# Two layers of sliding attention and an MLP mixer: the first group's w3 product in fp16, block 0's x centred by VectorE, and a new order

## The chip, the cores and the metric

The kernel runs on one core of one Trainium2 chip. The metric is device time in microseconds (us) of that core for one launch. Lower is better.

## The reference

x has 2048 rows (tokens) of 512 columns in fp32. Two different layers, A and B, are applied in turn, twice, with the same weights both times:

```python
x = A_x
x = x + A(LN(x), wqkv, wo)
x = x + B(LN(x), w1, w2, w3, w4)
x = x + A(LN(x), wqkv, wo)
x = x + B(LN(x), w1, w2, w3, w4)

def A(x, wqkv, wo):            # 32 heads of 16 columns
    q, k, v = split(x @ wqkv)  # 512 x 1536
    # row s attends to rows s, s-2, ..., s-14 (8 keys, those below 0 masked)
    return softmax(q . k[s - 2w] / 4) . v[s - 2w] @ wo

def B(x, w1, w2, w3, w4):      # called with LN(x), and normalises again
    h  = gelu(LN(x) @ w1)      # 512 x 512
    hs = shift(h) @ w2         # quarters of the columns shifted by +1, -1, +2, -2 rows
    x1 = x + hs
    return x1 + gelu(LN(x1) @ w3) @ w4   # 512 x 1792, 1792 x 512
```

LN subtracts the row's mean and divides by the root of its variance plus 1e-5; it has no gain or bias. All inputs and the output are fp32.

## The kernel before

**Tiles and stages.** The 2048 rows are four blocks of 512, and a block is four tiles of 128 rows. With two layers there are eight passes over a block, numbered n = 0 to 7 (0 to 3 are the blocks of the first layer). One pass goes through five stages, each a function of that name: `p1` (LN, transpose of x, the q, k, v products with wqkv), `p2` (attention, on VectorE with some help from GpSimd; `p2_unit` takes one or two of the four quarters of a block), `p3` (product with wo, residual, LN, product with w1, gelu, the row shift), `p4` (product with w2, residual, LN, transpose) and `p5` (w3, gelu, w4, residual). Because of the row shift a pass can finish only part of its rows: `p5` of n = 0 has three tiles, its last has five, the others four. `p5` walks over 14 chunks of 128 of the 1792 columns of w3; the result of a chunk's first (up) product goes through gelu and into the second (down) product, which adds up in PSUM (`acc`).

**Precision.** Nearly all products are three fp16 products in place of one fp32 product. Each operand is cut into a high half (its fp16 rounding) and a low half (the fp16 rounding of the remainder), and `HLS` lists the three pairs high-high, high-low and low-high:

```python
HLS = ((0, 0), (0, 1), (1, 0))
```

Weights are scaled per row by a power of two before the cut, with a factor found from their sum of squares (`small_weight` for wqkv, wo, w1, w2; `big_pair` for w3 and w4). The halves of w3 and w4 are kept in DRAM (`w34_d`) and each `p5` loads them chunk by chunk. Two places use plain fp32 matmuls: the qkv product of block 0 (`p1_quarters`, which takes wqkv quarter by quarter as it arrives), and the whole of `p5` for the first pass (`n < PLAIN`, `PLAIN = 1`, function `plain_chunk`), whose w3 and w4 are read in fp32 from the inputs.

**Normalisation at the start.** `p1_norm` takes mean and variance of an x tile on VectorE (BN_STATS, BN_AGGR). For block 0 GpSimd then does three small operations (`power`: variance plus eps, the power -1/2, minus mean times root) and one pass over the tile, x times root minus mean times root (`normed`). TensorE transposes the tile (`turn_f32`), ScalarE copies it out of PSUM, and the qkv products follow. ScalarE's copy of q out of PSUM multiplies by 1/4.

**Transposes elsewhere.** A tile that needs its fp16 halves transposed goes either through TensorE (`turn_pe`, `turn_f32`) or as a transposing DMA (`turn_dma`: ScalarE writes the fp16 copy, VectorE or GpSimd the remainder, the SP queue issues the transpose). `BY_DMA` says from which n on a stage uses the DMA.

**What sets the order.** The program is first recorded as a list of operations, each with a sort key, an engine (some with a second one) and the buffers it reads and writes. `PLACES` is a table with one integer per operation, which replaces the key; `OTHER` names the operations that run on their second engine. `plan` walks the operations in that order, assigns a slot of a pool to each buffer (`mm` and `acc` four PSUM banks each, `w` eight weight slots, `g` five, `f32` six) and emits the instructions. All instructions are recorded through one helper, `InOrder.issue`, so every row of the profile names its line, L338. Each engine runs its own list strictly in that order, and waits when an input is not there. Nearly all DMAs are issued from the SP queue, whose list is in the table's order too.

**Loads at the start.** The loads that are not needed for block 0's qkv products carry `begun`, a dependence on the copy of block 0's first quarter. `small_weight` loads a 512 x 512 weight with one DMA. `big_pair` converts two chunks of w3 and the same two of w4 together, seven times; one operation, `scales`, waits for all of them and computes the factors `s_w3`, `c_g`, `s_w4` that undo the scaling.

## Time and the profile before

| | us |
|---|---|
| median of 3 runs | 1144.0 (1142.68 to 1894.58) |
| the profiled execution | 1145.03 |
| its span, first to last instruction | 1143.2 |
| TensorE (PE) busy | 1124.1 (98%) |
| VectorE (DVE) busy | 862.6 (75%) |
| ScalarE (ACT) busy | 618.6 (54%) |
| GpSimd (POOL) busy | 417.9 (37%) |
| mean granted TensorE clock | 0.997 |

"Span" is the time between the first and the last instruction of one execution; the profiled execution's own time is 1.8 us longer. PE are the matmuls, PEld the weight loads beside them, SPq the SP queue's DMA issues. A row of the timeline has the start and the duration in us, the engine, the operation, "out<-in" by the program's names, partitions x elements, and in brackets the idle time ahead of it and what ended that. A row of a group has count, busy time in us, mean ns of one, and idle time ahead. A row of the waits has who waits for whom: the total in us, how often, the longest. A row of the busy windows has the stretch, its length, and the busy time of PE, PEld, DVE, ACT and POOL in it with the count of instructions, then the granted clock, the busy share of the DMA engines, and GB/s.

### The profile page before, as it was taken

How to read it: one execution, taken by the hardware profiler on the slowest of the kernel's cores; microseconds unless marked ns; L12 is line 12 of the kernel's file. 1: busy time of each engine (PE TensorE's matmuls, PEld its weight loads, DVE VectorE, ACT ScalarE, POOL GpSimd, SP SyncE). 2: the span in 40 equal slices, each digit the busy share in tenths (PEclk: the TensorE clock that was granted, in tenths of full speed). 3: DMA queues.
4: the chain of work that ended last, by engine and by line, in shares of the span. 5: the costliest groups of instructions: out<-in, count | busy, mean ns of one | idle time of the engine just before them, and what ended most of it. 6: DMA issues, size and time to landing. Idle time of an engine off the chain costs nothing.

```text
span 1143.2 us, 15112 instructions
## 1 busy us (share of the span) xinstructions
PE 1124.1 (98%) x5190; PEld 532.4 (47%) x5190; DVE 862.6 (75%) x919; ACT 618.6 (54%) x1089; POOL 417.9 (37%) x596
## 2 busy tenths in 40 slices
PE   8989999999999999999999999999999999999998
PEld 6544445554444444444444444444444444444554
DVE  4989899997899998988888888378986888323212
ACT  4766785247863565464654565354555554535321
POOL 4342364125652571135534353252324342322000
PEclk9999999999999999999999999999999999999999
DMA  6988989997989669974679756596687865524322
GB/s 175 217 205 215 223 216 259 256 238 182 265 234 222 162 161 211 244 187 121 161 182 230 192 136 166 128 237 177 154 206 166 199 168 158 113 75 112 100 88 79
DMA packets 249165, 206.37 MB, mean 181 GB/s; under 512 B 131032, under 2 KB 192472, under 8 KB 249088
## 3 DMA queue, kind: packets, MB, share of 16 engines
q1 hardware_dynamic: 247472, 203.63, 72.3%
q10 hardware_dynamic: 1616, 1.77, 0.5%
q8 instruction: 41, 0.67, 0.2%
q14 instruction: 36, 0.29, 0.1%
HBM read 132.64 MB, written 37.87 MB: 149 GB/s over the span
## 4 chain that ended last, share of the span: by engine, by line
PE 60%; ACT 2%; DVE 1%; issue 1%; POOL 1%; POOLq 0%; DVEq 0%; ACTq 0%
PE mm L338 42%; PE acc L338 18%; POOL small L338 1%; ACT f L338 1%; DVE L L338 0%; DVE prod L338 0%; ACT junk L338 0%; DVE f L338 0%; ACT L338 0%; ACT g L338 0%; ACT mm L338 0%; POOL f L338 0%; DVE x L338 0%; POOL o L338 0%; DVE h L338 0%
## 5 line engine op out<-in xcount | busy, mean ns | idle before, releaser
L338 PE MATMUL acc<-w,g 128*128 128x512 f16 (+1 forms) x1260 | 307.3, 394 | 0.0
L338 PE MATMUL mm<-nT,w 128*128 128x512 f16 (+1 forms) x1288 | 301.7, 389 | 0.8 <-ACT f L338 0.8
L338 PE MATMUL mm<-wq_hl,xt 128*128 128x512 f16 x1008 | 226.8, 381 | 3.2 <-DMA xt<-f 2.3
L338 ACT ACTIVATE mm<-mm,s_w 128x512 f32<-128x512 f32 (+1 forms) x144 | 89.7, 628 | 195.0 <-PE mm L338 194.7
L338 PEld LDWEIGHTS <-w 128*128 128x128 f16 x1344 | 125.2, 98 | 142.2 <-issue 1.0
L338 PEld LDWEIGHTS <-g 128*128 128x128 f16 x1176 | 114.7, 98 | 137.5
L338 DVE TENSOR_TENSOR prod<-kv,L 128x2048 f32<-128x2048 f32 x64 | 148.7, 2325 | 13.6 <-POOL o L338 12.2
L338 PEld LDWEIGHTS <-xt 128*128 128x128 f16 x1008 | 98.8, 98 | 122.5 <-issue 4.8
L338 DVE TENSOR_REDUCE L<-prod 128x128 f32<-128x2048 f32 x64 | 146.2, 2284 | 1.2
L338 POOL TENSOR_SCALAR small<-small 128x1 f32<-128x1 f32 (+1 forms) x200 | 88.8, 444 | 137.8 <-ACT junk L338 123.8
L338 DVE TENSOR_TENSOR prod<-kv,q 128x2048 f32<-128x2048 f32 x58 | 134.3, 2316 | 3.7 <-DMA q<-q_d 1.9
L338 DVE TENSOR_TENSOR prod<-prod 128x512 f32<-128x512 f32 (+2 forms) x109 | 111.5, 1026 | 2.7
L338 POOL TENSOR_TENSOR g<-f,g 128x512 f16<-128x512 f32 x39 | 54.8, 1409 | 117.8 <-ACT g L338 69.2
L338 DVE SCALAR_TENSOR_TENSOR g<-mm,c_g,g 128x512 f16<-128x512 f32 x56 | 41.5, 745 | 63.7 <-ACT g L338 63.7
L338 PE MATMUL mm<-w_hl,h 128*128 128x512 f16 x384 | 85.7, 379 | 1.1 <-POOL h L338 1.1
L338 PE MATMUL mm<-nT,w_hl 128*128 128x512 f16 x384 | 86.5, 379 | 0.0
L338 POOL TENSOR_TENSOR small<-small,nhalf 128x1 f32<-128x1 f32 (+1 forms) x104 | 72.3, 695 | 8.7
L338 PE MATMUL mm<-wo_hl,oT 128*128 128x512 f16 x336 | 74.3, 379 | 0.0
L338 POOL TENSOR_TENSOR prod<-prod 128x512 f32<-128x512 f32 (+1 forms) x24 | 30.5, 1271 | 105.9 <-DVE prod L338 99.4
L338 ACT ACTIVATE ev<-mm,s_kv 128x512 f32<-128x512 f32 x56 | 38.1, 681 | 54.8 <-PE mm L338 40.0
L338 ACT ACTIVATE g<-mm,c_g 128x512 f16<-128x512 f32 x98 | 66.6, 684 | 1.9
L338 PEld LDWEIGHTS <-oT 128*128 128x128 f16 x426 | 41.5, 98 | 49.0 <-issue 0.6
(188 smaller groups left out, 1217.8 us busy)
## 6 DMA issues: line engine op xcount, KB each, us to landing
w<-w SPq DMA_DIRECT2D x196, 256.0 KB
kv<-kv_d SPq DMA_DIRECT2D x112, 352.0 KB
w<-in_B_w_dram SPq DMA_DIRECT2D x56, 256.0 KB
kv_d<-ev SPq DMA_DIRECT2D x112, 128.0 KB
q_d<-ev SPq DMA_DIRECT2D x28, 256.0 KB
w<-g SPq DMA_DIRECT2D x28, 256.0 KB
q<-q_d SPq DMA_DIRECT2D x28, 256.0 KB
x<-x SPq DMA_DIRECT2D x26, 256.0 KB
```

What stands on the lines that cost most here:

```text
L338: i = f(*a, **k).ins
```

## The change

The numbers of `PLACES` and `OTHER` are all new, and several functions change:

- **The first pass's up product** (`p5`, `n < PLAIN`) takes the halves of w3 from `w34_d`, as the other passes do, and makes 12 fp16 matmuls of 384 columns for a chunk (4 row chunks of w3, three pairs each) where 4 fp32 matmuls stood. Its gelu undoes the scaling with `s_w3`. The down product stays fp32 with w4 from the input (`plain_down`).
- **Block 0's second normalised x** (`p4`, n = 0) is therefore cut into fp16 halves and transposed by DMA (`BY_DMA["p4"]` 1 to 0), not by TensorE in fp32.
- **Block 0's first x** is centred only: x minus mean, by VectorE (or GpSimd, by `OTHER`; one tile of four is). The root is not applied to x but in ScalarE's copies of q, k and v out of PSUM, as a scale per row.
- **The loads** that waited for `begun` wait for nothing; `small_weight` loads in four DMAs of 128 rows each.
- **w3 and w4 are converted apart**, in groups of four chunks (4, 4, 4, 2), w3 first (`big_four` for `big_pair`); `s_w3` comes from each group by itself.
- **Block 0's attention** takes its quarters in pairs, as the others do (`PAIRED` 1 to 0).
- **The planner** has other numbers for some costs and a finer rule for the port that VectorE and GpSimd share. It sets the order and the slots, nothing else.

```diff
-BY_DMA = {"p1": 1, "p2": 1, "p3": 1, "p4": 1}
+BY_DMA = {"p1": 1, "p2": 1, "p3": 1, "p4": 0}
...
-            power(key, mvt, ve, r, i, k, EPS * k, mvt, -1.0, nb, 0, 1)
+            def root():
+                G.tensor_scalar(ve.t[:, s], mvt.t[:, 1:2], k, EPS * k, ALU.mult, ALU.add)
+                G.tensor_tensor(r.t[:, s], ve.t[:, s], nhalf[:, :1], ALU.pow)
+                G.tensor_scalar(nb.t[:, s], r.t[:, s], DH ** -0.5, None, ALU.mult)
+            gp(key, 1.2, root, [(mvt, 1)], [(ve, i), (r, i), (nb, i)], cls="tiny")
...
+        if b == 0 and l == 0:
+            op(key, [(DVE, 0.5, lambda: V.tensor_scalar(nr.t, src(), mvt.t[:, :1], None, ALU.subtract), None),
+                     (POOL, 0.77, lambda: G.tensor_scalar(nr.t, src(), mvt.t[:, :1], 1.0, ALU.subtract, ALU.mult), None)],
+               [xr, (mvt, 0)], [nr, (xt, "n")])
+            turn_f32(key, nr, xt, [xt], lambda: f32v(xt.t, D).rearrange("p (c t) -> p c t", c=NC))
+            return xt, (r, i), (nb, i)
         if l == 0:
             normed(key, nr, src, r, nb, i, [xr], [(xt, "n")], [(POOL, 0.77, G, None)])
-            if b == 0:
-                turn_f32(key, nr, xt, [xt], lambda: f32v(xt.t, D).rearrange("p (c t) -> p c t", c=NC))
-                return xt
...
                             A.activation(d.t[:, f:f + P], ps.t[:, P * m:P * (m + 1)], AF.Copy,
-                                         scale=1.0 if k else DH ** -0.5)
+                                         scale=xts[i][1 if k else 2][0].t[:, i:i + 1])
...
-        dma(key - 3.0, lambda: v().rearrange("p (c f) -> p c f", c=NC),
-            lambda: wd.rearrange("(c p) f -> p c f", p=P), [], [(st, c) for c in range(NC)], 4.0, begun)
+        for c in range(NC):
+            dma(key - 3.0, lambda c=c: v()[:, D * c:D * (c + 1)], lambda c=c: wd[P * c:P * (c + 1), :],
+                [], [(st, c)], 1.0, begun)
...
+        if k == 0:
+            def inverse():
+                v = s_w3.t[:, cs[0]:cs[0] + len(cs)]
+                V.tensor_scalar(v, iv4.t, SN, None, ALU.mult)
+                V.reciprocal(v, v)
+            dve(key, 0.3, inverse, [iv4], [(s_w3, j)])
...
-    iv = [big_pair(c, KW + 0.6 + 0.2 * c) for c in range(NP)]
+    iv = [big_four(k, j, KW + 0.6 + 0.4 * k + 0.1 * j) for k in range(2) for j in range(len(FOURS))]
...
-    PAIRED = 1
+    PAIRED = 0
...
-        def up():
-            for k in range(NC):
-                T.matmul(ps.t[:, :P * K], f32v(w3.t, D)[:, P * k:P * (k + 1)],
-                         f32v(nT.t, NC * D)[:, D * k:D * k + P * K], start=(k == 0), stop=(k == NC - 1))
...
         act(key, 0.15 + 0.115 * K, lambda: A.activation(f32v(g.t, D)[:, :P * K], ps.t[:, :P * K],
-                                                       AF.Gelu_apprx_tanh, scale=1.0 / SN), [ps], [g], cls=GELU)
+                                                       AF.Gelu_apprx_tanh, scale=s_w3.t[:, c:c + 1]),
+            [ps, (s_w3, c // 4)], [g], cls=GELU)
...
-            if n < PLAIN:
-                dma(key - 0.003, lambda w3=w3: f32v(w3.t, D).rearrange("p (k f) -> p k f", k=NC),
-                    lambda c=c: w3_d[:, P * c:P * (c + 1)].rearrange("(k p) f -> p k f", p=P), [], [w3], 1.0, begun)
-                dma(key - 0.0015, lambda w4=w4: f32v(w4.t, D), lambda c=c: w4_d[P * c:P * (c + 1), :],
-                    [], [w4], 1.0, begun)
-                plain_chunk(c, key, w3, w4, acc, x2T[n][0])
-                continue
...
+                if n < PLAIN:
+                    dma(key - 0.0015, lambda w4=w4: f32v(w4.t, D), lambda c=c: w4_d[P * c:P * (c + 1), :],
+                        [], [w4], 1.0, begun)
+                    plain_down(c, key, ps, w4, acc)
+                    continue
```

How the order moves, at three places. In the rows, L338 of before is L347 of the changed kernel, and the number behind a name is that of its buffer.

VectorE at the start of the program, before the change: `w` holds an x tile of block 0, `mx` its statistics, `ev` a constant.

```order
L338 BN_STATS mx_163<-w_162 128x6
L338 BN_AGGR mx_164<-mx_163 128x2
L338 MEMSET ev_165 16x512
L338 BN_STATS mx_169<-w_166 128x6
L338 BN_AGGR mx_170<-mx_169 128x2
L338 BN_STATS mx_163<-w_167 128x6
L338 BN_AGGR mx_169<-mx_163 128x2
L338 BN_STATS mx_164<-w_176 128x6
L338 BN_AGGR mx_163<-mx_164 128x2
L338 SCALAR_TENSOR_TENSOR wq_hl,ssq<-nT_168 128x3x128 x2
```

The same place after the change; `f` is the centred tile.

```order
L347 BN_STATS mx_157<-w_155 128x6
L347 BN_AGGR mx_158<-mx_157 128x2
L347 TENSOR_SCALAR f_159<-w_155,mx_158 128x512
L347 BN_STATS mx_161<-w_156 128x6
L347 BN_AGGR mx_162<-mx_161 128x2
L347 TENSOR_SCALAR f_164<-w_156,mx_162 128x512
L347 BN_STATS mx_157<-w_166 128x6
L347 BN_AGGR mx_161<-mx_157 128x2
L347 BN_STATS mx_158<-w_170 128x6
L347 BN_AGGR mx_157<-mx_158 128x2
L347 TENSOR_SCALAR f_175<-w_170,mx_157 128x512
```

Three of the four x tiles now get their subtraction (`f<-w,mx`) on VectorE, each behind its own mean; the `ev` memset has gone behind the first squares of wqkv (`ssq`), and those squares are of 384 columns where a 128-column pair stood first.

VectorE from the scale of wqkv (`inv_q`) to the first attention product (`prod<-kv,q`), before: `wq_hl<-...` are the remainders of wqkv's pieces, `s_kv` and `s_q` the factors that undo its scale.

```order
L338 TENSOR_REDUCE mx_170<-mm_68 128x1
L338 TENSOR_SCALAR mx_170<-mx_170 128x1
L338 TENSOR_SCALAR inv_q<-inv_q 128x1 x2
L338 TENSOR_SCALAR s_kv<-inv_q 128x1
L338 RECIPROCAL s_kv<-s_kv 128x1
L338 TENSOR_SCALAR s_q<-s_kv 128x1
L338 SCALAR_TENSOR_TENSOR wq_hl<-nT_168,inv_q,wq_hl 128x3x128 x3
L338 SCALAR_TENSOR_TENSOR wq_hl<-h_175,inv_q,wq_hl 128x3x384 x2
L338 SCALAR_TENSOR_TENSOR wq_hl<-h_184,inv_q,wq_hl 128x3x384 x2
L338 TENSOR_TENSOR prod_198<-kv_181,q_180 128x2048
```

After:

```order
L347 TENSOR_REDUCE mx_158<-mm_68 128x1
L347 TENSOR_SCALAR mx_158<-mx_158 128x1
L347 TENSOR_SCALAR inv_q<-inv_q 128x1 x2
L347 TENSOR_TENSOR prod_189<-kv_169,q_168 128x2048
L347 SCALAR_TENSOR_TENSOR wq_hl<-h_174,inv_q,wq_hl 128x3x384
L347 TENSOR_TENSOR prod_191<-kv_169,q_168 128x2048
L347 SCALAR_TENSOR_TENSOR wq_hl<-nT_163,inv_q,wq_hl 128x3x128
L347 SCALAR_TENSOR_TENSOR wq_hl<-h_171,inv_q,wq_hl 128x3x384 x2
L347 SCALAR_TENSOR_TENSOR wq_hl<-nT_163,inv_q,wq_hl 128x3x128
L347 TENSOR_REDUCE L_190<-prod_189 128x16x8
```

The first attention product stood behind seven remainders of wqkv; now it stands behind the scale itself, and the remainders stand among the attention's products.

The SP queue where block 0's `p4` and the first `p5` come, before: `w<-in_B_w_dram 128x4x128` is a chunk of w3 from the input, `kv_d` and `q_d` are block 3's k, v and q going to DRAM, `w_0_113` and the like a chunk's halves in `w34_d`.

```order
L338 DMA w_162<-in_B_w_dram 128x4x128
L338 DMA w_193<-in_B_w_dram 128x4x128
L338 DMA w_188<-in_B_w_dram 128x4x128
L338 DMA x_195<-in_A_x_dram 64x512 x2
L338 DMA q_d_111<-ev_208 128x4x128
L338 DMA w_1_114<-g_174 128x1024
L338 DMA w_197<-in_B_w_dram 128x512
L338 DMA w_192<-in_B_w_dram 128x4x128
L338 DMA w_193<-in_B_w_dram 128x512
L338 DMA kv_181<-kv_d_109 64x1408 x2
L338 DMA w_0_113<-g_172 128x1024
```

After:

```order
L347 DMA_TRANSPOSE xt_194<-f_193 128x8x128
L347 DMA w_9_122<-g_176 128x1024
L347 DMA kv_d_109<-ev_200 64x4x128
L347 DMA w_8_121<-g_165 128x1024
L347 DMA w_166<-w_5_118 128x1024
L347 DMA kv_d_109<-ev_200 64x4x128
L347 DMA_TRANSPOSE nT_163<-f_172 128x8x128
L347 DMA_TRANSPOSE nT_163<-f_175 128x8x128
L347 DMA_TRANSPOSE nT_163<-f_193 128x8x128
L347 DMA w_156<-w_3_116 128x1024
L347 DMA w_177<-in_B_w_dram 128x512
L347 DMA q_d_111<-ev_200 128x4x128
```

The loads of w3 from the input are gone; in their place stand loads of the halves from `w34_d` (`w_166<-w_5_118`, `w_156<-w_3_116`), each behind its chunk's own store, and three transposing DMAs (`nT<-f`) of block 0's second normalised x.

116 lines of the change are left out of this document (60 added, 56 removed), and 289 rows, old and new, of tables (OTHER, PLACES).

## Prediction

> **What bounds the kernel now.** I read the page's busy shares first, then TensorE's list of waits, then the busy time by stage, and last single instructions at the places where TensorE has no slack.
>
> ```profile
> PE 1124.1 (98%) x5190; PEld 532.4 (47%) x5190; DVE 862.6 (75%) x919; ACT 618.6 (54%) x1089; POOL 417.9 (37%) x596
> ...
> PE mm L338 <- ACT f L338: 3.1, 4, 1.4
> PE mm L338 <- POOL f L338: 2.3, 2, 1.7
> PE mm L338 <- DMA xt<-f: 2.3, 2, 1.6
> PE mm L338 <- ACT ev L338: 2.1, 2, 1.9
> PE mm L338 <- ACT junk L338: 1.3, 1, 1.3
> PE mm L338 <- POOL h L338: 1.1, 1, 1.1
> ```
>
> TensorE works for 1124.1 of 1143.2 us, and no releaser cost it more than 3.1 us in total. So the end moves with TensorE's own work, and little is to be had from waits. But the average hides that VectorE is nearly as full early on:
>
> ```profile
> 25.00:50.00 25.00, 25.00 (x81) 14.66 (x80) 24.36 (x24) 22.77 (x62) 9.34 (x15) 1.00 0.79 220
> ...
> 150.00:185.00 35.00, 35.00 (x172) 16.89 (x171) 34.83 (x35) 30.21 (x51) 21.69 (x33) 1.00 0.96 237
> 185.00:225.00 40.00, 40.00 (x113) 21.30 (x112) 39.02 (x30) 9.72 (x15) 10.38 (x7) 1.00 0.97 252
> 225.00:273.00 48.00, 48.00 (x160) 23.35 (x159) 43.73 (x46) 25.20 (x48) 16.47 (x25) 1.00 0.98 245
> ```
>
> The third figure after the stretch's length is VectorE: 34.8 of 35, 39.0 of 40, 43.7 of 48 us, with the DMA engines (last but one) at 96 to 98%. This is where the changed matmuls are (185 to 273 us). TensorE and VectorE both set the pace here; a TensorE that gets 9 us shorter needs its inputs 9 us sooner.
>
> **TensorE's work.** The rows of matmuls by shape:
>
> ```profile
> L338 PE MATMUL mm<-nT,w 128*128 128x512 f16 x1176 | 264.0, 379 | 0.8 <-ACT f L338 0.8
> L338 PE MATMUL mm<-nT,w 128*128 128x384 f32 x112 | 37.8, 486 | 0.0
> L338 PE MATMUL mm<-xt,w 128*128 128x128 f16 x168 | 11.2, 219 | 0.0
> L338 PE MATMUL mm<-ident,prod 128*128 128x128 f32 x12 | 1.8, 273 | 0.0
> ```
>
> The second row is what goes: 14 chunks of fp32 w3 product, two records to a matmul, 37.8 us. In its place come 14 x 12 = 168 fp16 matmuls of 384 columns. There is no such row; busy time over count gives 0.2245 us at 512 columns and 0.0667 at 128, on the line between them 0.172 at 384, so 28.9 us: **-8.9**. Three transposes of block 0's second LayerNorm leave TensorE for the DMA queue: four records of 0.15 us each, three times, **-1.5**. One more small product with `ones` (eight groups of weights instead of seven) is +0.15. The down products stay fp32. Sum **-10.2 us**, known to some tenths.
>
> **The start.**
>
> ```profile
> 7.45 0.66 PE L338 MATMUL mm<-ident,f 128*128 128x128 f32 x4 [1.40 <-ACT f L338]
> 9.95 2.86 PE L338 MATMUL mm<-nT,g 128*128 128x128 f32 x16 [0.54 <-DMA nT<-in_A_wqkv_dram]
> 18.43 0.66 PE L338 MATMUL mm<-ident,f 128*128 128x128 f32 x4 [1.67 <-POOL f L338]
> ...
> 14.01 0.18 DVE L338 BATCH_NORM_AGGREGATE mx<-mx 128x2 f32<-128x6 f32 x1
> ...
> 16.63 1.74 POOL L338 TENSOR_SCALAR f<-w,small 128x512 f32<-128x512 f32 x1
> ```
>
> The last x tile has its mean at 14.19, but three small POOL steps and a POOL pass over the tile end at 18.37, and TensorE waits 1.67 us. With the centring on VectorE the tile is ready one VectorE pass after its mean. Three of the four centrings run there; no such row exists; by its nearest, the POOL pass at its shortest 0.76, I take 0.5 us (0.3 to 0.8). The root is then needed by ScalarE's copy of q, k, v only, after the products. The 1.40 at the first tile is mostly followed by the weights' DMA (0.54 at 9.95), so I count only the 1.67: **-1.7** (0 to -3.1).
>
> **A new wait where the products begin.** Block 0's normalised x now goes ScalarE fp16 copy, VectorE or POOL remainder, DMA transpose, instead of TensorE and one ScalarE copy. In the new order 36 matmuls of block 3's qkv stand between the last W2 product and the first w3 product: 36 x 0.2158 = 7.8 us of cover (0.2158 is the spacing 7.77/36 of the W2 row below). The path to be covered:
>
> ```profile
> 168.17 7.93 PE L338 MATMUL mm<-w_hl,h 128*128 128x512 f16 x36
> ...
> 176.66 0.75 DVE L338 SCALAR_TENSOR_TENSOR f<-mm,s_w,f 128x512 f32<-128x512 f32 x1
> ...
> 179.66 0.80 ACT L338 ACTIVATE f<-f,small 128x512 f32<-128x512 f32 x1
> ...
> L338 ACT ACTIVATE f<-f 128x512 f16<-128x512 f32 x56 | 34.9, 627 | 3.9 <-POOL f L338 1.5 <-DMA oT<-f 1.1
> L338 POOL TENSOR_TENSOR f<-f,f 128x512 f16<-128x512 f32 x20 | 23.6, 1180 | 29.5 <-ACT f L338 29.5
> ...
> 119.06 1.28 SPq L338 DMA_TRANSPOSE xt<-f  x1
> ...
> 122.72 5.35 PE L338 MATMUL mm<-wq_hl,xt 128*128 128x512 f16 x24 [0.65 <-DMA xt<-f]
> ```
>
> The last W2 product ends at about 176.0 and the normalised tile is there at 180.46: 4.5 us. Then 0.63 copy, 1.18 on POOL (two of the three remainders stand there), 1.28 to issue, and from the end of an issue to the matmul that waited for it 122.72 - 120.34 = 2.4: 10.0 us against 7.8. I take **+2.0**; the lower end is 0 (SP's issue overlaps), the upper 5, by the slowest transposed tile:
>
> ```profile
> 77.13 1.80 SPq L338 DMA_TRANSPOSE xt<-f  x1
> ...
> 84.63 7.95 PE L338 MATMUL mm<-wq_hl,xt 128*128 128x512 f16 x36 [1.62 <-DMA xt<-f]
> ```
>
> (5.7 us after its issue). A wait has a second price: after 1.90 us of it the next 24 matmuls took 6.91 us, where 24 take 5.34 (247.29), with a granted clock of 0.57:
>
> ```profile
> 61.93 0.38 PE L338 MATMUL mm<-ss_w,ones 128*128 128x1 f32 x2 [1.90 <-ACT ev L338]
> 62.50 6.91 PE L338 MATMUL mm<-wq_hl,xt 128*128 128x512 f16 x24 [0.19 <-ACT ev L338]
> ...
> 247.29 5.34 PE L338 MATMUL mm<-wo_hl,oT 128*128 128x512 f16 x24
> ...
> 62.00:64.00 2.00, 1.81 (x6) 0.79 (x7) 0.00 (x0) 2.00 (x7) 0.00 (x0) 0.57 0.63 168
> ```
>
> That is 1.6 us, which I keep for the range, since the 1.62 at 84.63 cost nothing after it. The Trainium skill, "TensorE: Matmul & The Clock Gate", section "Part 1: The HAM clock gate (the "warmup" mystery)", halves the clock only after an idle window of about 3.4 us; by it a wait of 2.0 costs 2.0. The trace disagrees: 1.90 was enough, and the sum would be 1.6 us later.
>
> **VectorE at block 1's attention.** In the old order TensorE takes up block 1's Wo product just as its input lands:
>
> ```profile
> 241.18 0.75 DVE L338 SCALAR_TENSOR_TENSOR f<-o,c_o,f 128x512 f16<-128x512 f32 x1 [0.18 <-ACT f L338]
> ...
> 242.40 2.33 SPq L338 DMA_TRANSPOSE oT<-f  x1
> ```
>
> Issue until 244.73, and 2.4 to land gives 247.1, against a start at 247.29: slack 0.2. Ahead of this product the new order holds the same 13 up products, one more down product (+2.6), and no transposes: 13 x (37.8 - 28.9)/14 = 8.3, so 8.3 + 1.5 - 2.6 = 7.2 us less; with -1.7 and +2.0 TensorE is there 6.9 us sooner. VectorE before the end of that attention gets +2.2 (two squares of 1152 columns instead of one of 384 and ScalarE's), +1.5 (centrings), +1.5 (`s_w3` and the eighth group) and +2.3 (adds that POOL had), and loses 4.9 (remainders of weights, moved to POOL); pairing block 0's softmax is about even. Net +2.5. It has idle time to set against that:
>
> ```profile
> 32.68 2.28 DVE L338 TENSOR_TENSOR prod<-kv,q 128x2048 f32<-128x2048 f32 x1
> ```
>
> The first attention product stood behind 7 us of wqkv remainders and started at 32.68; now it stands ahead of them and can start near 25, with VectorE's idle 16.8 of the first 25 us falling to about 12.5. So its chain ends 4.3 - 2.5 = 1.8 us sooner if all its other idle time stays (15 us from 25 to 242, mostly waits for ScalarE, TensorE and DMA), and TensorE waits 5.1; if a third of that goes, nothing. I take **+2.0** (0 to 5.1). Past this point VectorE's list up to the next block's h is shorter than it was by 3 to 5 us, so the remaining saving is not taken back.
>
> Hidden, and costed at nothing: small weights in quarters (the same bytes; three more issues each on a queue whose issues are 0.4 to 0.6 us), the paired softmax, and w3's conversions before w4's: four groups with 14 tiles precede the first w3 product, where three with 12 did, and the last two tiles are used some 50 us later. The stage's cover for them is TensorE's filler; without it one late chunk costs a landing, 5.7 us.
>
> **The sum.** -10.2 - 1.7 + 2.0 + 2.0 = **-7.9 us**. The profiled execution took 1145.03 us (span 1143.2 and 1.8 around it), so 1137.1; the runs' median is 1144.0, 1.0 below, so **1136**.
>
> **Rivals.**
> - VectorE takes it all. For: slack of 0.2 us at 247, and 34.8 of 35 us busy. Against: about 15 us of its own idle time before. Only its 1.8 us and the 3 us of TensorE's work behind Wo would be saved, less 2 for a second such meeting: 3, so 1141; 0 to 4 gives 1140 to 1144.
> - The early waits go too. The new order may close 61.9 and 84.6 (1.90 + 1.6 of slow clock + 1.62) and need no new wait: -10.2 - 1.7 - 5.1 = -17, 1127. For: the waits are small and named. Against: TensorE now runs up to tighter producers.
> - Slower: w3's round trip. Each w3 chunk is now read back from DRAM after its own store, on one SP queue, with the DMA engines at 97%. Before, its source was ready from the start. A chunk pair lasts 5.2 us on TensorE and now about 4.6; if three reloads miss by a landing each, 3 x 5.7 = 17, net +9: 1153. It decides from the point where the reloads lag more than the eight w slots hold. Against: the same 256 KB per chunk, in longer runs than w3's 512-byte rows.
> - The change not doing what it says: three fp16 products being no cheaper than fp32 would leave -1.5 and the new waits, 1146. The rows above speak against it.
>
> The Trainium skill, "SBUF — State Buffer", section "Who interferes with whom", has VectorE and GpSimd share a port pair as an exclusive lock, so work moved to POOL is paid by waiting:
>
> ```profile
> L338 POOL TENSOR_TENSOR inv_p<-mx,nhalf x7: 1013/1395/3002, 71.1 to 312.1; 128x4 f32<-128x4 f32 x7
> ```
>
> The same root took 1.01 to 3.00 us here. By the rule the root in the path at the first w3 product could add 2 us: that sum would be 1138.
>
> **Chances.** Forecast (1131 to 1140) 0.57; VectorE takes it (1140 to 1144) 0.16; early waits go (below 1131) 0.15; slower than before by any of the last two 0.12. The range takes in the second and third: **1126 to 1147**. About 2% is what a measurement of this kernel can tell from no change, 23 us: faster by that needs below 1121, which even the third case misses, 0.03; slower, above 1167, needs several late reloads, 0.04; within, 0.93.
>
> **What would show it.** Right: an f16 row of 168 matmuls at 384 columns with 28 to 30 us; no POOL pass before the fourth tile's transposes; a wait of about 2 us on the DMA of nT ahead of the first w3 product; a wait at block 1's Wo on the DMA of oT. Wrong: waits on the DMA of w inside the first group's products; VectorE waits instead of TensorE's at block 1; or the sum of TensorE's idle time moving by more than 8 us either way.

## The result, and the profile after

The changed kernel takes 1152.16 us (median of 4 runs, 1150.28 to 1154.4) against 1144.2 of the kernel before on the same chip: a ratio of **1.0075** (95% interval 1.005 to 1.01). It is slower by 8 us; the forecast was 1136, faster by 8. The profiled execution took 1154.4 us with a span of 1152.6, 9.4 longer than before.

The page of the changed kernel, busy times and the chain that ended last:

```profile
PE 1119.7 (97%) x5236; PEld 528.5 (46%) x5236; DVE 879.9 (76%) x907; ACT 615.5 (53%) x1076; POOL 529.3 (46%) x631
...
PE 56%; DVE 16%; POOL 9%; DMA 7%; ACT 6%; issue 4%; SPq 2%; POOLq 0%; DVEq 0%; ACTq 0%
```

TensorE's busy time fell by 4.4 us only (1124.1 to 1119.7), not by 10.2, and its idle time rose from 19.1 (1143.2 - 1124.1) to 32.9. GpSimd works 111.4 us longer, and VectorE 17.3 us longer with 12 instructions fewer. The chain before the change is followed back only to 403 us. From there to the end it held 15.9 us of VectorE and 8.6 of GpSimd; now it holds 108 and 33 there, and in a second profiled execution of the changed kernel (`e16_new_again` below) 66 and 22.

TensorE's list of waits (for whom; total us, times, longest):

```profile
PE mm L347 <- DMA nT<-f: 7.2, 4, 4.9
PE mm L347 <- DVE h L347: 4.6, 4, 2.9
PE acc L347 <- ACT g L347: 3.1, 1, 3.1
PE mm L347 <- DMA xt<-f: 2.1, 2, 1.6
PE mm L347 <- DVE g L347: 1.8, 2, 1.3
PE mm L347 <- ACT ev L347: 1.7, 3, 0.8
PE acc L347 <- DMA w<-w: 1.4, 1, 1.4
```

The longest entry before was 3.1 us in four parts. New are a wait of 4.9 where the first w3 product starts, one of 2.9 for VectorE's `h`, and one of 3.1 for a gelu.

Busy windows, cut at points of TensorE's work (first w3 product, Wo product of block 1, first `p5` product of block 1, end of the first layer's last w1 product, end). After:

```profile
0.00:187.00 187.00, 174.09 (x795) 92.95 (x796) 162.50 (x193) 134.93 (x270) 124.33 (x150) 0.99 0.87 223
187.00:245.00 58.00, 58.00 (x237) 29.42 (x236) 54.65 (x50) 18.40 (x33) 11.44 (x11) 0.97 1.00 246
245.00:320.00 75.00, 69.97 (x303) 31.80 (x302) 63.29 (x87) 51.45 (x96) 53.63 (x68) 0.98 0.83 211
320.00:535.00 215.00, 207.70 (x959) 93.40 (x958) 187.39 (x164) 111.78 (x178) 99.55 (x110) 1.00 0.78 190
535.00:1152.60 617.60, 609.92 (x2948) 280.90 (x2945) 412.10 (x418) 298.95 (x499) 240.32 (x295) 1.00 0.62 153
```

The same stretches before:

```profile
0.00:185.00 185.00, 174.44 (x804) 92.70 (x805) 153.90 (x189) 132.02 (x272) 77.70 (x135) 0.99 0.87 214
185.00:247.00 62.00, 62.00 (x179) 32.61 (x178) 60.22 (x51) 16.39 (x30) 14.62 (x9) 1.00 0.97 240
247.00:319.00 72.00, 70.71 (x305) 32.58 (x303) 60.66 (x90) 56.72 (x108) 41.23 (x57) 1.00 0.90 231
319.00:526.00 207.00, 206.31 (x957) 93.31 (x956) 186.12 (x177) 113.64 (x181) 81.10 (x103) 1.00 0.83 199
526.00:1143.20 617.20, 610.68 (x2953) 281.24 (x2951) 401.67 (x416) 299.82 (x498) 203.26 (x295) 1.00 0.61 152
```

Read by row, the stretch lengths differ by +2, -4, +3, +8 and +0.4. Up to the first w3 product GpSimd has 46.6 us more to do and VectorE 8.6, part of it work on attention that came later in the old order; TensorE waits 4.9 us at the end of this stretch. The second stretch holds 13 of the 14 fp16 up products and is 4 us shorter. By its rows the whole product takes 30.8 us in place of 37.8, 7.0 less. At a steady pace a chunk takes 1.95 us from start to start instead of 2.58, which would be 8.8 less for the 14, but the first 48 matmuls, right behind the wait of 4.9, took 9.64 us instead of 7.8, at a granted clock of 0.82. In the third stretch TensorE's idle time goes from 1.3 to 5.0, and in the fourth from 0.7 to 7.3, with its work there the same within 1.4 us. In the second profiled execution the fourth stretch is 5.1 us longer than before, with 3.8 of idle time: the size varies, the direction does not.

Groups of instructions after (count, busy us, mean ns, idle ahead):

```profile
L347 PE MATMUL mm<-nT,w 128*128 128x384 f16 x168 | 30.8, 339 | 4.9 <-DMA nT<-f 4.9
L347 POOL TENSOR_SCALAR small<-small 128x1 f32<-128x1 f32 x188 | 111.0, 591 | 154.4 <-ACT junk L347 141.1
L347 POOL TENSOR_TENSOR small<-small,nhalf 128x1 f32<-128x1 f32 x96 | 72.5, 756 | 8.0
L347 DVE TENSOR_TENSOR prod<-kv,q 128x2048 f32<-128x2048 f32 x58 | 141.1, 2433 | 5.5 <-DMA kv<-kv_d 4.0 <-DMA kv<-kv 1.0 <-POOL o L347 0.2
L347 DVE TENSOR_TENSOR o<-prod 128x256 f32<-128x256 f32 x41 | 22.5, 549 | 8.6 <-POOL prod L347 7.7
```

Before:

```profile
L338 POOL TENSOR_SCALAR small<-small 128x1 f32<-128x1 f32 x184 | 83.2, 452 | 136.4 <-ACT junk L338 123.8
L338 POOL TENSOR_TENSOR small<-small,nhalf 128x1 f32<-128x1 f32 x96 | 63.8, 664 | 8.0
L338 DVE TENSOR_TENSOR prod<-kv,q 128x2048 f32<-128x2048 f32 x58 | 134.3, 2316 | 3.7 <-DMA q<-q_d 1.9 <-DMA kv<-kv_d 1.2 <-POOL o L338 0.2
L338 DVE TENSOR_TENSOR o<-prod 128x256 f32<-128x256 f32 x36 | 15.8, 442 | 2.6 <-POOL prod L338 1.7
```

The same instructions on the same operands last longer on both engines. GpSimd's small operations are the roots of the LayerNorms, three in a chain (`small<-small`, the power with `nhalf`, `small<-small`), 96 chains in a run. Undisturbed a chain lasts 1.2 us. Taken operation by operation, 26 of 96 chains lasted over 2 us before and 43 after (40 in the second execution); the sum went from 167.2 to 204.3 us. (Counts of 29 and 48 in the expectations below come from rows that merge two neighbours, and are a little high.) What that does on the way to TensorE is seen at two of the new waits, the first w3 product and the wait for `h`. The timeline there, after:

```profile
174.91 2.29 DVE L347 TENSOR_TENSOR prod<-kv,q 128x2048 f32<-128x2048 f32 x1
...
175.14 2.47 POOL L347 TENSOR_SCALAR small<-small 128x1 f32<-128x1 f32 x2
...
177.37 0.81 ACT L347 ACTIVATE f<-f,small 128x512 f32<-128x512 f32 x1 [2.99 <-POOL small L347]
...
186.82 9.64 PE L347 MATMUL mm<-nT,w 128*128 128x384 f16 x48 [4.93 <-DMA nT<-f]
...
406.43 2.29 DVE L347 TENSOR_TENSOR prod<-kv,L 128x2048 f32<-128x2048 f32 x1 [0.84 <-POOL o L347]
...
406.49 2.29 POOL L347 TENSOR_SCALAR small<-small 128x1 f32<-128x1 f32 x1
408.86 1.53 POOL L347 TENSOR_TENSOR small<-small,nhalf 128x1 f32<-128x1 f32 x1
410.49 0.27 POOL L347 TENSOR_SCALAR small<-small 128x1 f32<-128x1 f32 x1
...
410.79 0.81 ACT L347 ACTIVATE prod<-x,small 128x512 f32<-128x512 f32 x1 [5.03 <-POOL small L347]
...
417.45 5.34 PE L347 MATMUL mm<-wq_hl,xt 128*128 128x512 f16 x24 [2.89 <-DVE h L347]
```

And before, at the second place:

```profile
404.24 0.19 POOL L338 TENSOR_SCALAR small<-small 128x1 f32<-128x1 f32 x1 [0.26 <-ACT junk L338]
404.51 0.55 POOL L338 TENSOR_TENSOR small<-small,nhalf 128x1 f32<-128x1 f32 x1
405.16 0.27 POOL L338 TENSOR_SCALAR small<-small 128x1 f32<-128x1 f32 x1
```

A GpSimd operation of 0.19 us on one column lasts 2.29 when VectorE's attention product started 0.06 us earlier (406.43 and 406.49), and ends with it. The row at 175.14 holds operations of two chains. The last operation of the first chain, 0.26 us undisturbed, lasts 2.19 and ends with the product; the second chain starts behind it, at 177.42, and takes 1.2 us. So at the first place ScalarE's normalised tile comes 2.99 us late, then its copy, remainder and transpose, and TensorE waits 4.93. At the second ScalarE waits 5.03 us for the root, and behind that wait stand, in its fixed order, the gelus that feed `h`. Before the change VectorE ran sums of `acc` and x at this place, which read PSUM, and the root was done in 1.2 us.

### The profile page after: what moved, and what is told of

Its sections match the earlier page's. It is cut to its first block, busy times and chain, and to the rows that moved or that the text cites. A ratio compares the mean times of both kernels' runs of the same rounds, so it can differ in the third digit from the quotient of the medians.

```text
span 1152.6 us, 15231 instructions
## 1 busy us (share of the span) xinstructions
PE 1119.7 (97%) x5236; PEld 528.5 (46%) x5236; DVE 879.9 (76%) x907; ACT 615.5 (53%) x1076; POOL 529.3 (46%) x631
## 4 chain that ended last, share of the span: by engine, by line
PE 56%; DVE 16%; POOL 9%; DMA 7%; ACT 6%; issue 4%; SPq 2%; POOLq 0%; DVEq 0%; ACTq 0%
PE mm L347 38%; PE acc L347 18%; DVE prod L347 8%; POOL small L347 6%; DVE L L347 3%; ACT f L347 2%; SPq L347 2%; DVE f L347 1%; ACT junk L347 1%; DMA kv<-x 1%; DMA x<-x 1%; DMA q_d<-ev 1%; DMA nT<-f 1%; POOL f L347 1%; DVE g L347 1%
## 5 line engine op out<-in xcount | busy, mean ns | idle before, releaser
L347 PE MATMUL acc<-w,g 128*128 128x512 f16 (+1 forms) x1260 | 309.0, 395 | 5.9 <-ACT g L347 3.1
L347 PE MATMUL mm<-nT,w 128*128 128x512 f16 (+1 forms) x1344 | 295.2, 374 | 7.2 <-DMA nT<-f 5.4
L347 PE MATMUL mm<-wq_hl,xt 128*128 128x512 f16 x1008 | 225.5, 379 | 7.7 <-DVE h L347 3.7
L347 PEld LDWEIGHTS <-w 128*128 128x128 f16 x1512 | 141.9, 98 | 165.6 <-issue 16.0
L347 ACT ACTIVATE mm<-mm,s_w 128x512 f32<-128x512 f32 (+1 forms) x144 | 89.6, 628 | 200.1 <-PE mm L347 199.9
L347 POOL TENSOR_SCALAR small<-small 128x1 f32<-128x1 f32 (+1 forms) x204 | 121.4, 595 | 155.8 <-ACT junk L347 141.1
L347 PEld LDWEIGHTS <-g 128*128 128x128 f16 x1176 | 114.5, 98 | 141.1 <-issue 1.9
L347 DVE TENSOR_TENSOR prod<-kv,L 128x2048 f32<-128x2048 f32 x64 | 150.2, 2347 | 8.1 <-POOL o L347 5.6
L347 PEld LDWEIGHTS <-xt 128*128 128x128 f16 x1008 | 98.5, 98 | 125.4 <-DMA xt<-f 6.0
L347 DVE TENSOR_REDUCE L<-prod 128x128 f32<-128x2048 f32 x64 | 146.0, 2284 | 1.3
L347 DVE TENSOR_TENSOR prod<-kv,q 128x2048 f32<-128x2048 f32 x58 | 141.1, 2433 | 5.5 <-DMA kv<-kv_d 4.0
L347 DVE TENSOR_TENSOR prod<-prod 128x1024 f32<-128x1024 f32 (+2 forms) x111 | 118.1, 1067 | 5.3 <-ACT prod L347 2.5
L347 PE MATMUL mm<-nT,w_hl 128*128 128x512 f16 x384 | 86.4, 379 | 1.8 <-DMA nT<-f 1.8
L347 PE MATMUL mm<-w_hl,h 128*128 128x512 f16 x384 | 86.0, 379 | 0.0
L347 POOL TENSOR_TENSOR small<-small,nhalf 128x1 f32<-128x1 f32 (+1 forms) x104 | 81.7, 786 | 8.7
L347 DVE SCALAR_TENSOR_TENSOR g<-mm,c_g,g 128x512 f16<-128x512 f32 x56 | 41.3, 744 | 57.3 <-ACT g L347 57.3
L347 POOL TENSOR_TENSOR g<-f,g 128x512 f16<-128x512 f32 x34 | 49.5, 1459 | 58.4 <-ACT g L347 29.4
L347 PE MATMUL mm<-wo_hl,oT 128*128 128x512 f16 x336 | 74.3, 379 | 0.0
L347 ACT ACTIVATE g<-mm,c_g 128x512 f16<-128x512 f32 x98 | 66.3, 684 | 1.9
L347 PEld LDWEIGHTS <-oT 128*128 128x128 f16 x426 | 41.4, 98 | 50.9 <-ACT oT L347 1.1
L347 PEld LDWEIGHTS <-w_hl 128*128 128x128 f16 x384 | 37.5, 98 | 47.1 <-issue 2.2
L347 PEld LDWEIGHTS <-h 128*128 128x128 f16 x384 | 37.6, 98 | 45.3 <-POOL h L347 0.2
```

Source lines behind the costliest of these rows:

```text
L347: i = f(*a, **k).ins
```

## The experiments

Times are medians; the kernel before was run beside each, at 1144 to 1145 us. "New order" stands for the whole new arrangement: `PLACES`, `OTHER`, and all edits but the one named. The line of the helper in the rows differs from kernel to kernel.

**The product alone.** Is the saving there, and does the kernel take it? Two kernels: the old order with a cheap up product (operands coarser, as the expectation says), and the new order with the fp32 product.

```diff
-            for k in range(NC):
-                T.matmul(ps.t[:, :P * K], f32v(w3.t, D)[:, P * k:P * (k + 1)],
-                         f32v(nT.t, NC * D)[:, D * k:D * k + P * K], start=(k == 0), stop=(k == NC - 1))
+            hi = w3.t.bitcast(BF16).rearrange("p (f two) -> p f two", two=2)[:, :, 1]
+            for m in range(3 * NC):
+                k = m // 3
+                T.matmul(ps.t[:, :P * K], hi[:, P * k:P * (k + 1)],
+                         nT.t.bitcast(BF16)[:, D * k:D * k + P * K], start=(m == 0), stop=(m == 3 * NC - 1))
```

> The kernel before, in its old order, with only the first pass's 14 up products made cheap: 12 bf16 matmuls of 384 columns each (upper halves of the fp32 words of w3, same count and width as the three fp16 products), so the first group's values are rounded coarsely; loads, transposes and everything else as before. Theory 'port' (the new order lets VectorE's long two-input operations hold up GpSimd's three small root operations, and the products' gain is real): 1144.2 - 8.9 = 1135, between 1133 and 1138. Theory 'VectorE' (VectorE's list sets the pace, so cheaper products are worth little in any order): 1141 to 1144. Theory 'w3 trip' (reloading w3's halves from DRAM costs the time): also 1135, since nothing is reloaded here.

Measured 1143.58, ratio 0.9994 (0.9977 to 1.0012): no gain, as the expectation has it for the theory 'VectorE'. The timeline of that kernel where part of the gain goes:

```profile
226.04 0.72 ACT L338 ACTIVATE prod<-o,c_o 128x512 f16<-128x512 f32 x1 [10.44 <-DVE o L338]
...
228.04 1.23 ACT L338 ACTIVATE g<-mm 128x384 f32<-128x384 f32 x3
...
228.94 5.49 PE L338 MATMUL acc<-w,g 128*128 128x512 f32 x6 [4.81 <-ACT g L338]
```

TensorE waits 4.81 us for a gelu. Its matmul was long done; the gelu stands on ScalarE behind an operation that needs `o` of block 1's attention, and VectorE ran that attention with hardly a pause. The six matmuls behind the wait then take 5.49 us where six took 2.74 at 210.39. So VectorE's list is one limit of the old order there; a later run measures how much of the loss it is.

The second kernel puts the transposes by TensorE and the fp32 product with w3 from the input back into the new order.

```diff
-            dma(key - 0.003, lambda w3=w3: w3.t, lambda c=c: w34_d[c][:, 0].rearrange("p a f -> p (a f)"),
-                [(w34, (c, 0))], [w3], 1.0)
+            if n < PLAIN:
+                dma(key - 0.003, lambda w3=w3: f32v(w3.t, D).rearrange("p (k f) -> p k f", k=NC),
+                    lambda c=c: w3_d[:, P * c:P * (c + 1)].rearrange("(k p) f -> p k f", p=P), [], [w3], 1.0, begun)
...
+                    if n < PLAIN:
+                        for k in range(NC):
+                            T.matmul(ps.t[:, :wd], f32v(w3.t, D)[:, P * k:P * (k + 1)],
+                                     f32v(nT.t, NC * D)[:, D * k:D * k + wd], start=(k == 0), stop=(k == NC - 1))
+                        return
```

> The changed kernel, in its new order, with the w3 edit alone taken back: fp32 up products from w3 in the input, block 0's second normalised x transposed by TensorE. TensorE has 10.4 us more work. 'port': the wait of 4.9 us at the first up product shrinks to about 2 (the roots still stand behind VectorE's product, but copy, remainder and transposing DMA go), so 1152 + 10.4 - 3 - about 3 of later waits that the longer products cover = 1157, from 1154 to 1160. 'VectorE': 1152 to 1153, since TensorE only waits less. 'w3 trip': 1146 or less, near the kernel before.

Measured 1161.26, ratio 1.0147 (1.0115 to 1.0179). The changed kernel is 9.1 us below it (1161.26 - 1152.16), and 8.2 by the two ratios, each of which is known to some 3 us. Like for like the forecast was -8.4: -8.9 for the product, -1.5 for the transposes, which this kernel takes back too, +0.15, and +2.0 for the wait that comes with the DMA. So the w3 edit is worth what was forecast, as far as these intervals can tell, and the new order without it costs **16.4** (1161.26 - 1144.85). None of the expected times held; nearest is the theory that puts the loss on GpSimd's port (1154 to 1160). A late reload of w3 can't be the cause: this kernel reads w3 from the input and is slower still.

**Is VectorE the pace in the old order?** The cheap product again, with one VectorE add of block 1's attention cut from 128 columns to 16; and that cut alone.

```diff
-                    e.tensor_add(pv4()[:, :, 0:4], pv4()[:, :, 0:4], pv4()[:, :, 4:8])
+                    c = slice(0, 16 if n == 1 else P)
+                    e.tensor_add(pv4()[:, :, 0:4, c], pv4()[:, :, 0:4, c], pv4()[:, :, 4:8, c])
```

> The kernel before in its old order with the cheap up products (12 bf16 matmuls of 384 columns a chunk), and VectorE lightened: of the first of three pairwise additions of block 1's attention output only 16 of 128 columns are added (eight instructions of 1.23 us become about 0.2), so the values of block 1 are not the reference's. 'VectorE and ScalarE's order pace the first w3 stage': the wait of 4.8 us behind the attention's output goes, and the products' 8.9 us show: 1136 (1134 to 1138). 'Something else (DMA of w3 and w4, ScalarE)': 1142 to 1144, as without the lightening.

> The kernel before with only that lightening of VectorE, fp32 up products. 'VectorE paces only a shorter TensorE': TensorE had no idle time from 146 to 279 before, so nothing to win: 1143 to 1145. 'VectorE sets the time in any case': 1136 to 1138.

Together 1141.16, ratio 0.9971 (0.9959 to 0.9983); the cut alone 1144.9, 1.001 (0.9995 to 1.0024). VectorE's time there is worth nothing while the product is fp32, as expected, and 2.4 us once it is cheap (1143.58 to 1141.16; the intervals of the two ratios overlap a little): by this it paces only a shorter TensorE. The time of 1136 expected for the pair was missed. The wait for the gelu falls to 3.18 only, and of the product's 8.9 us some 3 show (1144.2 to 1141.16), so VectorE's time in that attention is shown for a part of the loss in the old order; the rest stays open. The same cut in the new order:

> The changed kernel with the lightened VectorE of the earlier pair: of the first of three additions of block 1's attention output only 16 of 128 columns are added, eight instructions, some 8 us less; the values of block 1 are not the reference's. 'VectorE paces the first w3 stage in the new order too': the waits at 265.8 and behind it shrink, 1146 to 1149. 'Roots and other chains': 1151 to 1153.

1153.08, ratio 1.0084 (1.0052 to 1.0117): no gain over the 1152.16, as expected by 'Roots and other chains'.

**Single places.** The first attention product that holds a root ahead of the first w3 product goes behind the first remainder; VectorE's list alone changes.

```diff
+        if o.seq == 587:
+            o.key = 670.5
```

> The changed kernel with one operation moved: VectorE's long product of block 1's attention that stands between block 0's second sums and the first remainder (174.91 in the trace) goes behind that remainder. 'port': the roots at 173.70 and 176.38 take 1.2 us instead of 2.7 and 2.2, the wait of 4.93 us at the first up product falls to 2 to 3, and the whole to 1149 to 1150, unless VectorE's 2.3 us of later attention take it back by 265. 'VectorE': the wait falls, the time stays at 1152 or grows by up to 2. 'w3 trip': wait and time unchanged.

1155.49, ratio 1.0096 (1.0069 to 1.0124). The first two root chains now take 1.70 and 1.20 us, but the third meets the moved product and takes 3.41; one operation of it:

```profile
177.19 2.49 POOL L349 TENSOR_SCALAR small<-small 128x1 f32<-128x1 f32 x1
...
177.34 2.28 DVE L349 TENSOR_TENSOR prod<-kv,q 128x2048 f32<-128x2048 f32 x1
```

The wait at the first w3 product only goes from 4.93 to 4.54, where 2 to 3 was expected. Next, five products held behind a root each, at four places, and the later two of these places alone:

```diff
+BEHIND = {587: 1014, 703: 1124, 871: 1690, 1385: 1834, 1387: 1858}
...
     for o in plan(op.ops, slots):
+        if o.seq in BEHIND:
+            V.tensor_scalar(seen.t, ROOTS[BEHIND[o.seq]](), 1.0, None, ALU.mult)
         o.fn()
```

> The changed kernel; at four places of TensorE's waits one long VectorE product is held back until GpSimd's roots ahead of it are done (five such products, by a read of the root of one column): 174.9 (also put behind the first remainder), 260.1, 406.4, and 495.1 with 501.0. 'Port, at the roots of TensorE's chains': the waits of 4.93, 3.06, 2.89 and 1.78 us fall to about 2.5, 1, 0.5 and 0.5, sum 8.2 less, and the time to 1144 (1142 to 1147). 'VectorE's throughput': the waits only move to later inputs from VectorE, time 1150 to 1156, as in the 53-read version but smaller.

> The same with only the last two places (406.4, and 495.1 with 501.0), which lie behind everything that concerns w3. 'Port': the waits of 2.89 and 1.78 us fall to 0.5 each, the time to 1148.5 (1147 to 1150). 'VectorE's throughput': 1152 to 1153.

1153.35, ratio 1.0082 (1.0063 to 1.0101), and 1152.2, 1.007 (1.0052 to 1.0088): no gain; the expected gains of 8 and 3.5 us did not come. At the first place two remainders on GpSimd now meet the held product (timeline of the first of the two):

```profile
178.82 3.97 POOL L350 TENSOR_TENSOR f<-f,f 128x512 f16<-128x512 f32 x2 [0.60 <-ACT f L350]
...
178.37 2.29 DVE L350 TENSOR_TENSOR prod<-kv,q 128x2048 f32<-128x2048 f32 x1
```

The row holds two remainders that take 1.16 us each alone. The first lasts 2.86 beside the product, the second 1.15 behind it. At the late place (`h`) the wait falls from 2.89 to 1.82, not to 0.5. TensorE's stretch from block 1's first `p5` product to the end of the layer's last w1 product lasts 212.0 and 213.0 us in these two kernels; the changed kernel's own two executions have 215.7 and 213.3, so a small gain there can't be told from its own variation. Then the remainders themselves go to VectorE, and two products behind them:

```diff
+for k in (1007, 1017):
+    OTHER[k] = 1 - OTHER.get(k, 0)
...
+        o.key = {587: 678.5, 588: 678.6}.get(o.seq, o.key)
```

> The changed kernel; at the first w3 product the two tile remainders that stand on GpSimd go to VectorE, and VectorE's long product (174.9) goes behind all three remainders, so that nothing on that chain meets it but the roots themselves, which are then 1.2 us each. 'Port on that chain': the wait of 4.93 us falls to 2 to 2.5, near the 2.0 that was forecast for it; the time falls by that, to 1150, if VectorE's delay of 3 to 4 us is not taken back, and stays at 1152 to 1154 if it is. 'Transposing DMA': the wait stays over 4.

1154.77, ratio 1.0087 (1.0059 to 1.0115). TensorE's rows of that kernel:

```profile
184.30 9.64 PE L352 MATMUL mm<-nT,w 128*128 128x384 f16 x48 [2.23 <-DMA nT<-f]
210.86 3.14 PE L352 MATMUL mm<-nT,w 128*128 128x384 f16 x12 [2.05 <-DMA w<-w]
...
268.00 2.84 PE L352 MATMUL acc<-w,g 128*128 128x512 f32 x6 [3.06 <-ACT g L352]
```

The wait falls to 2.23 as worked out, and TensorE starts 2.5 us sooner; at 210.86 it waits 2.05 for a chunk of w3 and later for the gelu as before. The time is that expected if VectorE's delay is not taken back. None of the single waits tried sets the end.

**Guards everywhere.** All of VectorE's long products wait for the last root ahead, through 53 tiny reads.

```diff
     for o in plan(op.ops, slots):
+        if o.seq in ROOTS:
+            wait.append(ROOTS[o.seq])
+        e, d, _, cls = o.alts[OTHER.get(o.seq, 0)]
+        if e == DVE and cls == "lock" and d > 1.0:
+            for v in wait[-1:]:
+                V.tensor_scalar(seen.t, v(), 1.0, None, ALU.mult)
+            wait = []
         o.fn()
```

> The changed kernel in which VectorE's long two-input operations (over 1 us) first read the result of the last GpSimd root that stands ahead of them in the order, 53 tiny reads in all, so that none of them starts while such a root is still to come. 'port': of 96 roots hardly any takes over 2 us (48 do now), GpSimd's busy time falls from 529 by about 60 us, TensorE's idle time from 32.9 to about 22, the time to about 1143, with 5 us either way, since VectorE now waits instead in places. 'VectorE': 1155 to 1165, since VectorE loses the waits and the reads. 'w3 trip': no fall, the waits on nT and w stay.

1185.76, ratio 1.0367 (1.0334 to 1.04). The roots get much of what they were to get (16 of 96 over 2 us, GpSimd's busy time down by 38 to 491.1, where 60 was expected), and the kernel loses 33.6 us, far more than either theory had: here VectorE's waiting costs more than the short roots are worth.

**GpSimd's share.** In the old order 20 operations go from VectorE to GpSimd by `OTHER` (remainders, attention outputs, residual adds); beside it the same 20 stay on VectorE, cut short.

> The kernel before in its old order, with 20 operations handed from VectorE to GpSimd without moving them, about what the change hands over: 6 remainders of w3 and w4, 7 remainders of transposed tiles, 3 of attention outputs, 4 residual additions, spread over the first 540 us. VectorE loses 20 x 0.72 = 14.5 us of work, GpSimd gets some 36 us. 'Contention' (work given to GpSimd beside VectorE's two-input operations is paid by both): VectorE's busy time falls by less than half of 14.5, GpSimd's rises by 50 or more, roots over 2 us go from 29 of 96 to 35 or more, the time rises by 5 to 12 us, to 1149 to 1156. 'VectorE's throughput alone': VectorE's busy time falls by 14 and the time stays at 1142 to 1145.

> The kernel before in its old order; the same 20 operations that the run 'more pool' handed to GpSimd stay on VectorE and are cut short (a fill with zero and 16 columns of the remainder or the addition), so the low halves and four residuals are not the reference's. VectorE gets the relief, GpSimd nothing. 'GpSimd's share costs' (the 8 us of the run 'more pool' are paid for GpSimd's work beside VectorE): VectorE's busy time falls by 8 to 13 us, the time stays at 1142 to 1145. 'Any disturbance of the order costs': the time rises here too, to 1148 or more.

```diff
+for k in [211, 229, 250, 274, 298, 328, 519, 603, 759, 795, 884, 1013, 1165, 1187, 1302, 1489, 1545, 1670, 1839, 1893]:
+    OTHER[k] = 1 - OTHER.get(k, 0)
```

And of the second kernel, for the weights' remainders (the others likewise):

```diff
+        if len(op.ops) in SHORT:
+            c = slice(0, 16)
+            alts = [(DVE, 0.4, lambda: (V.memset(lo(), 0.0), V.scalar_tensor_tensor(
+                lo()[:, c], src()[:, c], scale, hi()[:, c], ALU.mult, ALU.subtract)), "lock")]
```

1151.78, ratio 1.0067 (1.0041 to 1.0093), and 1142.44, 0.9985 (0.9972 to 0.9998). The pages, handed over first:

```profile
PE 1128.1 (98%) x5190; PEld 533.4 (46%) x5190; DVE 861.2 (75%) x899; ACT 619.1 (54%) x1089; POOL 457.7 (40%) x625
```

cut short:

```profile
PE 1123.6 (98%) x5190; PEld 532.9 (47%) x5190; DVE 860.2 (75%) x935; ACT 618.4 (54%) x1089; POOL 421.2 (37%) x596
```

Twenty operations of about 0.7 us leave VectorE, some 14 us, and its busy time falls by 1.4 (862.6 to 861.2): by its rows the rest lasts some 12 us longer. In the second kernel the shortened operations and their fills still cost some 9 us, so it takes off only about 6, and VectorE's busy time falls by 2.4. So VectorE ends up about equally busy in both, and the 9.3 us between them is the price of having GpSimd do this work in an order that was made without it. That price includes more than the port: the same operation lasts longer on GpSimd (1.2 to 2.0 us against 0.72), and it stands in GpSimd's list ahead of other work. These parts weren't separated. The time 'Contention' expected came; its expectations for the roots (35 over 2 us; in that count there were 26, and 29 before) and for GpSimd (50 us more; it was 39.8) missed, and so did VectorE's busy time in the second kernel (8 to 13 less). So in the old order the price did not come through more late roots.

Where the time goes is plain. TensorE's stretch from block 1's Wo product to its first `p5` product lasts 71.83 us before, 77.24 with the work handed over and 71.83 with it cut short; the next stretch, to the end of the layer's last w1 product, 208.25, 211.18 and 208.25. These are the same two stretches in which the changed kernel loses.

The counterpart in the new order: 26 operations go back to VectorE; in another kernel GpSimd's 14 remainders of w3 and w4 are cut short, with the changed kernel run again beside it.

```diff
+for k in [197, 212, 213, 237, 238, 246, 259, 282, 285, 304, 309, 334, 486, 564, 731, 834, 1017, 1019, 1127, 1193, 1405, 1531, 1559, 1561, 1712, 1861]:
+    OTHER[k] = 1 - OTHER.get(k, 0)
```

```diff
         def by_pool():
+            if n == D:
+                c = slice(0, 16)
+                G.memset(lo(), 0.0)
+                G.tensor_sub(lo()[:, c], src()[:, c], hi()[:, c])
+                return
```

> The changed kernel in its new order, with 26 operations handed back from GpSimd without moving them: 6 remainders of w3 and w4, 6 high halves (to ScalarE), 7 remainders of transposed tiles, 3 of attention outputs, 4 residual additions, in the first 540 us. VectorE gets 14.5 us of work back. 'Contention': VectorE's busy time rises by less than half of that, GpSimd's falls by 50 or more, the time falls to 1146 to 1151. 'VectorE's throughput alone': VectorE's busy time rises by 14 and the time to 1158 or more.

> The changed kernel in its new order; GpSimd's 14 remainders of w3 and w4 (two passes each, 35 us in all, in nobody's chain to TensorE before some 50 us later) are cut to a fill with zero and 16 columns, so w3's and w4's low halves are not the reference's. 'GpSimd's share costs': GpSimd's busy time falls by 35 to 50, VectorE's by 3 to 8 (less waiting for the port), the time by 3 to 6, to 1146 to 1149. 'The order alone' (TensorE stands too close behind chains of small steps, whoever shares a port): 1151 to 1153.

> The changed kernel once more, unchanged, on the same chip as the two above, so that a difference of 3 us can be told: 1150 to 1154 by its four runs so far.

Given back: 1161.3, ratio 1.0145 (1.0114 to 1.0176), with GpSimd's busy time down by 43 to 486.3 and VectorE's up by 8.0 to 887.9. The 1146 to 1151 of 'Contention' was missed; the time fits the rival, 'VectorE's throughput alone' (1158 or more), though it expected 14 more on VectorE. Handing work over costs in the old order and giving it back costs in the new one. Another reading fits this too: each order was made for its own assignment, and any other assignment in it costs. The run with the 20 operations cut short speaks against that for a change that only removes work; for moved work it stays untested.

Cut short: 1148.94, 1.0044 (1.0028 to 1.0061), against 1153.27, 1.0082 (1.0063 to 1.01), for the changed kernel: 12.6 us less on GpSimd (511.7 against 524.3) are worth **4.3 us**, with VectorE's busy time the same (880.3 and 880.7). The time is within the 1146 to 1149 of "GpSimd's share costs"; that theory's busy times (35 to 50 us less on GpSimd, 3 to 8 on VectorE) were missed. The two profiles don't show where the gain is: TensorE's idle time is 31.9 against 29.8, and the chains over 2 us are 43 against 40.

## Why the prediction was wrong

**Right.** The w3 product: -8.4 forecast like for like, 8.2 to 9.1 measured in the new order; the stated row of 168 fp16 matmuls came with 30.8 us, slightly above 28 to 30. The centring takes 0.63 us (0.5). VectorE up to the end of block 1's attention output: its busy time there rises by 5.6 us (209.1 to 214.7) where 2.5 was worked out, it idles 13.3 of the first 25 us (12.5), and the output is there 1.2 us sooner (1.8). The remainders of weights did leave it. One small slip: four records of 0.15 us, three times, are 1.8 and not 1.5, but by the spacing of the rows 1.5 is right.

**Right by luck, or only in kind.** The wait on the DMA of `nT` at the first w3 product came, with 4.93 the upper end of the 0 to 5 given. The reason was the one that stands in the paragraph on the port and was kept out of the sum: the last operation of one root was held for 2.2 us by an attention product, and the next root queued behind it. The second price of a wait, also kept out of the sum, came too: 1.7 us of lower clock behind it.

The table has the lengths of TensorE's stretches, in us, between the same points of its work. In the last column stand the terms of the sum: up to the first w3 product the start, the transposes, the small product and the wait (-1.7 - 1.5 + 0.15 + 2.0), up to Wo 13 of 14 up products and one more down product (-8.3 + 2.6), then the rest of these and the wait at Wo (-0.6 - 2.6 + 2.0).

| TensorE's stretch | before | changed | second execution | change | forecast |
|---|---|---|---|---|---|
| to the first w3 product | 185.19 | 186.82 | 188.20 | +1.6 | -1.1 |
| to block 1's Wo product | 62.10 | 58.17 | 58.56 | -3.9 | -5.7 |
| to block 1's first `p5` product | 71.83 | 74.58 | 73.40 | +2.8 | -1.2 |
| to the end of the layer's last w1 product | 208.25 | 215.69 | 213.34 | +7.4 | 0 |
| to the end | 615.86 | 617.35 | 617.33 | +1.5 | 0 |

**The step that failed** is the one that closes the paragraph on VectorE at block 1's attention: "VectorE's list up to the next block's h is shorter than it was by 3 to 5 us, so the remaining saving is not taken back". It put everything behind block 1's Wo product at nothing. There the new order takes 11.7 us longer, against -1.2 by the sum: some 13 of the 17 us by which the profiled time missed. The list wasn't shorter either: between Wo and block 1's first `p5` product VectorE is busy 63.3 us instead of 60.7 and GpSimd 53.6 instead of 41.2. The kernel with the fp32 product in the new order has the same late stretches (215.9 and 617.3 us), so this loss belongs to the new order and not to the w3 product. TensorE's idle time rises there with waits for roots, gelus and `h`, which stand in fixed lists behind a VectorE and a GpSimd that now last longer beside each other.

What the sum left out is GpSimd's price. It counted the work that leaves VectorE and not what it costs on GpSimd and on what runs beside it. The 20 operations handed over in the old order show it: 9.3 us of time, in the same stretches. I read the rule of the Trainium skill, "SBUF — State Buffer", section "Who interferes with whom", as 2 us at one place; by it VectorE's operations with two SBUF inputs contend with GpSimd operations that read SBUF. The trace agrees with the rule (0.19 us became 2.29, until the product's end), but 43 of 96 roots, and remainders too, lasted longer, not one root.

Two smaller terms failed as well. The wait at the first w3 product was put at +2.0 and measured 4.93, with 1.7 us of lower clock on top. The -1.7 of the start did not show at block 0's W2 product: the wait of 1.67 at the fourth tile shrank to 0.7 or less in the traces of the new order, but other early waits took its place. The W2 product starts at 162.9 to 168.2 us in six traces of the old order and at 164.7 to 168.2 in nine of the new (later still with the guards and with 26 operations given back), with the same mean of 165.9.

The stated sign of being wrong that came was TensorE's idle time, which moved by 13.8 us and not by 8 at most. So the new order cost 16.4 us, where the forecast had -1.7 for the start and +4 for two new waits.

**Rivals.** "VectorE takes it all" was a rival for the new order. In the old order the cheap product did bring nothing (1143.58), of which VectorE's share is shown for 2.4 us. "Slower: w3's round trip" gave 1153, close to the result, by a mechanism that did not occur: the wait on w3's chunks appears inside the first group only where TensorE was made earlier (2.05 us). That the range's upper case came so near is luck. A wait at block 1's Wo did not come; TensorE reached it 2.3 us sooner (244.99 against 247.29), not 6.9.

**What stays open.** How the 16.4 us divide. Measured parts are GpSimd's share (9.3 us for 36.5 us of its work in the old order, 4.3 for 12.6 in the new) and the single waits, whose removal came back elsewhere each time. How much the new positions alone cost, at the old assignment, wasn't separated: giving 26 operations back also filled VectorE. Nor was it separated how much of GpSimd's price is the port, how much its longer operations, and how much an order made for another assignment. That ScalarE's gelu stands behind the attention's output explains the 4.81 us in the old order; moving it ahead wasn't tried.

## What to carry to other kernels

An engine that is busy for 37% to 46% of the span isn't free: before work is handed to GpSimd, look at which VectorE operations with two SBUF inputs will run beside it, since both then lasted longer here, and above all whether a tiny GpSimd operation in a chain towards the bounding engine starts beside one. A saving on the bounding engine is worth only what the fixed lists of the engines behind it can follow; here nearly all of a saving of 9 us on TensorE was taken back in the old order, 2.4 us of it by VectorE's attention. Compare lengths of the same stretch of TensorE's work between kernels before you name a place: here most of the loss lay far behind the place that the forecast looked at. Where removing single waits does not move the end, cut one engine's work short with all else unchanged: of the runs here these told most about the cause.
